# Output stores on GpSimd's software DMA queue, and a first w1 piece of half the size: attention with a soft mixture of experts

## The chip, the cores and the metric

The kernel runs on one core of a Trainium2 chip. The core has a matrix engine (PE, TensorE), three engines for elementwise work (DVE or VectorE, ACT or ScalarE, POOL or GpSimd), and SP (SyncE), which here only issues transfers and waits. Sixteen DMA engines move data between HBM and the on-chip memory SBUF. A transfer can be issued from SP, on a hardware queue, or from POOL, on a software queue, for which POOL itself writes the descriptors. The metric is the device time of one execution in microseconds (us); less is better.

## The reference

The input is `q`, `k`, `v` of shape (8 batches, 8 heads, 576 positions, 64), and weights `moe_phi` (512, 32), `moe_w1` (8, 512, 1024) and `moe_w2` (8, 1024, 512), all float32.

```python
# attention with a mask by head
scores = (q @ k.T) / sqrt(64)
mask_plain = (rel >= 0) & (rel < 32)                       # heads 0..3
mask_dil   = (rel >= 0) & (rel < 128) & (rel % 4 == 0)     # heads 4..7
x = softmax(where(mask, scores, -1e9)) @ v                 # -> (4608, 512)
# soft mixture of experts: 8 experts with 4 slots each
logits = x @ phi
slot_input = softmax(logits, axis=0).T @ x                 # 32 slots
for e in range(8):
    slot_out[e] = relu(slot_input[e] @ w1[e]) @ w2[e]
out = softmax(logits, axis=1) @ slot_out                   # (4608, 512) float32
```

The slots need the logits of all 4608 rows, so no row of the output can be made before the whole attention is done, the experts' weights have been used, and the slot outputs are known.

## The kernel before

The work falls into 16 halves. Half `i` is batch `i // 2` with four of its heads: the plain mask for even `i`, the dilated one for odd `i`. For each half three loads (`load_half`, line 329) bring k, q and v from HBM as float32 and cast them to bf16 on the way. They go into one of four staging sets. DVE turns them (T, line 467 or 473) into one of two working sets, PE computes scores (SC), ACT takes the exponential (EX, line 526), PE and ACT bring v into shape (TB and VE), PE multiplies by v (PV), and DVE normalizes (RC and NM, lines 588 and 592). After that PE and ACT make the transposed x (XT and XE), and once per batch the logits (LG), their exponentials (EXL), their transpose (ET and EE) and the sum for the slots (SI and SA).

The experts' weights are cast to bf16 by the loads too, with one exception. The first 256 rows of `w1[0]`, 1 MB, are read as float32 by SP's hardware queue (line 381) into the space where expert 4's w2 comes later, and ACT casts them in two instructions (line 386). All other weights come through POOL: w1 pieces (line 339), w2 pieces (line 347), and for experts 6 and 7 slabs of 256 columns (line 354), so that the first 256 output columns can be computed before the last slabs are there. `W_AFTER` says how many weight pieces follow the loads of each half on POOL's queue; the rest follow the last half.

The program is not written in the order in which it runs. Each instruction or group is an `op` of a planner (`Sched`) with an engine, a guessed duration, a priority and the buffers it reads and writes. `run` plays them through in modelled time and always takes a ready operation of the least priority value. That gives the order of instructions on each engine; the waits between engines are set by the buffers. A priority in the loop is `PERIOD` times the half's number plus an offset of its stage in `OFFS`. A transfer in the plan has a size and a rate.

Behind the loop come the experts: L1 (line 777) with w1, ReLU on ACT, a transpose, and L2 (line 815) with w2. Their sum goes to `o_so`, first columns 0 to 255, then 256 to 511 (line 837). The output is made in 9 groups of 512 rows: a matmul (`out_tile`, line 856), and an eviction from PSUM to SBUF with the row's scale on ACT (line 865) or DVE (line 868), by turns. `store` (line 876) then sends it to HBM. Groups 0 to 2 are stored in pieces of 256 KB with rows of 1 KB: six pieces of the left columns, then six of the right. Groups 3 to 8 are stored in 1 MB each, 8 KB to a partition. Each store waits for its evictions; SP, which issues them in order, waits for all of them at the end (line 936).

Of the kernel before, what the change touches and what calls it, by code (L numbers as in the profile page):

```python
# [7 lines left out]
ACTF = mybir.ActivationFunctionType  # L8
# [10 lines left out]
NH = 16  # L19


W_AFTER = [0, 1, 1, 1, 1, 1, 1, 1, 1, 1, 1, 1, 1, 1, 1, 99]
PERIOD = 13.0
NSTG = 4
PE_SLOW = 1.1

OFFS = dict(T=12.4, SC=5.3, EX=-0.3, MK=27.3, TB=-8.9, VE=-4.9, PV=-2.7, RC=-36.2, NM=-26.5,
            XT=8.5, XE=14.2, LG=-29.0, EXL=18.1, ET=28.8, EE=6.0, SI=34.4, SA=11.6)


class Buf:
# [22 lines left out]
class Sched:  # L54
# [8 lines left out]
    def op(self, eng, fn, dur, prio, reads=(), writes=(), rmw=(), after=(), banks=(), name="",  # L63
           kind="c", nbytes=0, rate=422e3, lag=0.0, sem=None, tail=False):
        o = Op()
        o.eng, o.fn, o.dur, o.prio, o.name = eng, fn, dur, prio, name
        o.kind, o.bytes, o.rate, o.lag, o.sem, o.tail = kind, nbytes, rate, lag, sem, tail
        o.deps, o.succ = set(), []
        o.banks, o.opens, o.ord = [], [], None
        o.seq = len(self.ops)  # L70
        for a in after:
            if a is not None:
                o.deps.add(a)
        for b in reads:
            o.deps.update(b.w)
            b.r.append(o)
        for b in writes:
            if b.r:
                b.prev = b.w + b.r
                b.w, b.r = [], []  # L80
            o.deps.update(b.prev)
            b.w.append(o)
        for b in rmw:
            o.deps.update(b.prev)
            o.deps.update(b.w)
            o.deps.update(b.r)
            b.w.append(o)
        for b in list(reads) + list(writes) + list(rmw) + list(banks):
            if isinstance(b, Bank) and b not in o.banks:
                o.banks.append(b)  # L90
                if b.left == 0:
                    o.opens.append(b)
                b.left += 1
        o.deps.discard(o)
        self.ops.append(o)
        return o
# [98 lines left out]
def bass_dilated_sliding_attn__then__soft_moe_slots_kernel(  # L195
# [15 lines left out]
    def take(n):  # L211
        o = top[0]
        top[0] = o + (n + 1) // 2 * 2
        return o

    o_w1 = take(8 * 4 * FF)
# [37 lines left out]
    def a(off, dims, p0=0, pn=128):  # L254
        return AP(ar, p0 * NBF + off, [[NBF, pn]] + dims)
# [4 lines left out]
    def af(off, dims, p0=0, pn=128):  # L260
        return AP(ar_f.tensor, (p0 * NBF + off) // 2, [[NBF // 2, pn]] + dims)
# [12 lines left out]
    op = sc.op  # L274
    PE, ACT, DVE, POOL, SP = "PE", "ACT", "DVE", "POOL", "SP"
    pe, act, dve, pool, spq = nc.tensor, nc.scalar, nc.vector, nc.gpsimd, nc.sync

    def pet(n, cols):
        return (40.0 + n * max(cols / 2.4, 27.0)) * PE_SLOW / 1000.0
# [21 lines left out]
    b_w1 = [Buf(f"w1{e}") for e in range(8)]  # L301
    b_w2 = [[Buf(f"w2{e}{s}") for s in range(2)] for e in range(8)]
# [5 lines left out]
    def w2off(e):  # L308
        return o_w2 + e * 8 * DM if e < 5 else o_stg + (e - 5) * 8 * DM


    def sem(n):
        return [nc.alloc_semaphore(n), 0]
# [4 lines left out]
    def dma_in(fn, nbytes, s, prio, name, **kw):  # L318
        o = op(POOL, fn, 0.6, prio, kind="dma", nbytes=nbytes, sem=s,
               name=name, **kw)  # L320
        loads[name] = o
        return o
# [12 lines left out]
    wq = []  # L335

    def w1_piece(e, hf, r0=0, n=2):
        def fn():
            return pool.dma_start(
                a(o_w1 + e * 4096 + hf * 2048 + 1024 * r0, [[1, 1024 * n]]),  # L340
                moe_w1[e, 256 * hf:256 * hf + 256, :].rearrange("(p two) f -> p (two f)", two=2)
                [:, 1024 * r0:1024 * (r0 + n)])
        return (fn, n << 19, f"w1_{e}{hf}", [b_w1[e]])
# [13 lines left out]
        return (fn, n << 17, f"w2s_{e}{s}{c0}", [b_w2[e][s] if n == 8 else b_w2h[c0 // 4][s]])  # L357

    for e in range(8):
        wq += [w1_piece(e, x) for x in range(e == 0, 2)]  # L360
    for e in range(6):
        wq += [w2_piece(e, 0), w2_piece(e, 4)]
    for s in range(2):
# [1 line left out]
    nw = [0]  # L365

    def load_w(n):
        for _ in range(n):
            if nw[0] >= len(wq):
                return  # L370
            fn, nb, name, wr = wq[nw[0]]
            e = int(name.split("_")[1][0])
            rd = []
            if name.startswith("w2") and e >= 5:
                rd = [x for y in b_stg for x in y]
            nw[0] += 1
            dma_in(fn, nb, sem("s_" + name), rate=384e3 if name[2] == "s" else 422e3,
                   lag=2.3 if name[:2] == "w2" else 0.8, prio= -100.0 if nw[0] < 2 else -80.0, name=name, writes=list(wr) + rd)


    op(SP, lambda: spq.dma_start(
        af(w2off(4), [[1, 2048]]),
        moe_w1[0, 0:256, :].rearrange("(p two) f -> p (two f)", two=2)), .1, -200.0,
       kind="dma", nbytes=1 << 20, sem=sem("s_w1f"), writes=b_w2[4], name="w1f")
    for x in range(2):
        op(ACT, lambda x=x: act.activation(
            a(o_w1 + 1024 * x, [[1, 1024]]), af(w2off(4) + 2048 * x, [[1, 1024]]), ACTF.Copy),
            1.1, -200.0, reads=b_w2[4], writes=[b_w1[0]], name=f"w1c{x}")


    def const_ops():
# [50 lines left out]
    for bb in [b_et, b_phis, b_htz, b_sit] + b_p + b_xd + [x for y in b_vb for x in y]:  # L442
# [4 lines left out]
       kind="dma", nbytes=65536, sem=sem("s_phi"), writes=[b_phst], name="phi")  # L447
    for g in range(2):
# [3 lines left out]
           reads=[b_phst], writes=[b_phis])  # L452


    def half(i):
        b, dl = i // 2, i % 2
        T0 = i * PERIOD
        st, kq = i % NSTG, i % 2
        pr = lambda s: T0 + OFFS[s]
        ok, oq, ov = (o_kqv[kq] + 1152 * j for j in range(3))  # L460
# [164 lines left out]
        for x in range(2):  # L625
            bank = Bank(f"xt{i}{x}")

            def xt_fn(x=x, bank=bank):
# [14 lines left out]
            n = 6 if not dl else (2 if x else 8)  # L643
            op(PE, xt_fn, pet(n, 128 if dl else 96), pr("XT") + 0.4 * x, reads=[bx, b_id], writes=[bank],
               name=f"XT{i}{x}")
            c = 2 * dl
# [94 lines left out]
    for i in range(NH):  # L741
        load_half(i)
        half(i)
        if i == 13:
            row_sums(0, 7, 15 * PERIOD)
    names = [w[2] for w in wq]
    load_w(99)
    dma_order, w_at = [], 0
    for i in range(NH):
        dma_order += [f"ld{i}{c}" for c in "kqv"]  # L750
        dma_order += names[w_at:w_at + W_AFTER[i]]
        w_at += W_AFTER[i]
    for x, y in zip(dma_order, dma_order[1:]):
# [7 lines left out]
       writes=[b_rcol], name="cs")  # L761
# [4 lines left out]
       reads=[b_siacc], writes=[b_sit], name="sit")  # L766
    row_sums(7, 9, T1 + 4)
    hs_ops = []
    for g in range(2):
        for x in range(2):  # L770
            bank = Bank(f"l1{g}{x}")

            def l1_fn(g=g, x=x, bank=bank):
# [10 lines left out]
               writes=[bank], name=f"L1{g}{x}")  # L784
# [3 lines left out]
                writes=[b_hsb[g][x], b_p[0], b_p[1]], name=f"RL{g}{x}"))  # L788
    for g in range(2):
        bank = Bank(f"ht{g}")  # L790

        def ht_fn(g=g, bank=bank):
# [10 lines left out]
           reads=[bank], writes=[b_htz], name=f"HE{g}")  # L803
# [5 lines left out]
    def l2(es, x, col, n, cs=range(8), bufs=None):  # L809
# [20 lines left out]
       name="SOx")  # L830
# [14 lines left out]
    store_ops = []  # L845
# [3 lines left out]
    def ostg(G):  # L849
        return o_w1 + 4096 * G if G < 8 else o_w2  # L850
# [21 lines left out]
    def store(G, c0, cw, prio, j0=0, n=4):  # L872
        rd = [b_og[G][j][s] for j in range(j0, j0 + n) for s in range(2)
              if c0 < 256 * (s + 1) and c0 + cw > 256 * s]
        dst = out[512 * G:512 * G + 512, c0:c0 + cw].rearrange("(p j) f -> p j f", j=4)[:, j0:j0 + n, :]
        store_ops.append(op(SP, lambda: spq.dma_start(
            dst, af(ostg(G) + 2 * (512 * j0 + c0), [[512, n], [1, cw]])), .1, prio, kind="dma",
            nbytes=128 * n * cw * 4, rate=347e3 if cw < 512 else 420e3,
            sem=sem(f"s_o{G}{c0}{j0}"), reads=rd, name=f"ST{G}{c0}{j0}"))

    T2 = T1 + 40
    for G in range(NA):
        for x in range(0, 4, 2):
            for j in (x, x + 1):
                out_tile(G, j, 0, 256, T1 + 20 + G + .25 * x)
            store(G, 0, 256, T1 + 20 + G + .25 * x + .2, x, 2)
    for G in range(NA):
        for x in range(0, 4, 2):
            for j in (x, x + 1):
                out_tile(G, j, 256, 256, T2 + 10 + G + .25 * x)  # L890
            store(G, 256, 256, T2 + 10 + G + .25 * x + .2, x, 2)
    for G in range(NA, 9):
        for j in range(4):
            out_tile(G, j, 0, 512, T2 + 10 + G)
        store(G, 0, 512, T2 + 10 + G + .5)
# [74 lines left out]
```

## Time and profile before

| What | Value |
|---|---|
| Time, median of 3 runs | 181.22 us (180.66 to 181.52) |
| The profiled execution's own time | 181.52 us |
| Its span, first to last instruction | 179.7 us |
| Busy: PE, DVE, ACT, POOL | 69%, 64%, 59%, 27% of the span |
| Software queue (loads by POOL) | 30.41 MB written, 14992 packets |
| Hardware queue (SP: w1 piece, phi, stores) | 10.55 MB, 4544 packets |
| HBM read, written | 61.93 MB, 9.44 MB |

The page divides the span into 40 slices of 4.5 us; a digit is the busy share of a slice in tenths. A row of a group or of the timeline names the line of the kernel, the engine, the operation, what it writes and reads, and how many there are. A `q` behind an engine's name means its instruction queue, where transfers are issued. Bytes are counted at the destination, so a load that casts float32 to bf16 counts half of what it reads.

### The profile page before, as it was taken

What the parts mean: (1) busy time and instruction counts of PE and PEld (TensorE: products, weight loads), DVE (VectorE), ACT (ScalarE), POOL (GpSimd) and SP (SyncE); (2) the same over time, 40 slices, a digit from 0 to 9 for tenths busy, and PEclk for the clock granted to TensorE, in tenths of its full rate; (3) what the DMA queues carried; (4) which work ended last, traced back from release to release, by engine and by line L of the source; (5) the groups of instructions that cost most, each with busy time, mean ns of one, the idle gap of its engine ahead of it and who ended that gap; (6) DMA issues with size and microseconds to landing.
All of it is one profiled execution on the core that took longest, in us unless ns stands there. A gap on an engine that the chain in (4) does not pass through costs nothing.

```text
span 179.7 us, 5277 instructions
## 1 busy us (share of the span) xinstructions
PE 123.6 (69%) x2220; PEld 83.7 (47%) x2220; DVE 114.5 (64%) x214; ACT 106.4 (59%) x168; POOL 49.0 (27%) x98
## 2 busy tenths in 40 slices
PE   0018867977889789789689889885696088897000
PEld 0005645755666566566467567673343025531000
DVE  6897779979698698798599599460100013599000
ACT  2406598697799689688678788764141013498000
POOL 7559841432332333232930000930000000000000
PEclk9999999999999999999999999997569969999655
DMA  5999999999999999999999999999999998999994
GB/s 190 233 210 208 216 208 212 212 210 211 215 209 212 214 209 211 214 211 209 214 211 210 214 211 213 215 216 212 215 210 214 196 197 122 330 326 418 410 430 191
DMA packets 19559, 41.30 MB, mean 230 GB/s; under 512 B 1872, under 2 KB 9040, under 8 KB 18640
## 3 DMA queue, kind: packets, MB, share of 16 engines
q0 software_dynamic: 14992, 30.41, 89.7%
q1 hardware_dynamic: 4544, 10.55, 15.5%
q8 instruction: 18, 0.29, 0.6%
q14 instruction: 5, 0.04, 0.1%
HBM read 61.93 MB, written 9.44 MB: 397 GB/s over the span
## 4 chain that ended last, share of the span: by engine, by line
DMA 58%; DVE 19%; PE 10%; issue 3%; ACT 1%; DVEq 0%; POOL 0%; POOLq 0%
DMA ar<-in_k_dram 41%; DMA ar<-in_moe_w_dram 17%; DVE ar L868 5%; DVE ar L467 5%; PE ps L815 5%; DVE ar L592 2%; PE ps L487 2%; DVE ar L427 2%; PE ps L856 1%; DVE ar L432 1%; PE ps L494 1%; PE ps L548 1%; ACT ar L648 1%; ACT ar L526 1%; DVE ar L473 1%
## 5 line engine op out<-in xcount | busy, mean ns | idle before, releaser
L467 DVE STREAM_TRANSPOSE ar<-ar 128x576 uint32<-128x576 uint32 x40 | 48.9, 1244 | 10.1 <-DMA ar<-in_k_dram 10.0
L526 ACT ACTIVATE ar<-ps 128x1152 bf16<-128x1152 f32 (+1 forms) x32 | 38.1, 1190 | 19.8 <-PE ps L511 10.6
L487 PE MATMUL ps<-ar 128*128 128x320 bf16 (+1 forms) x128 | 22.8, 302 | 15.8 <-DVE ar L467 12.7
L554 ACT ACTIVATE ar<-ps 128x768 bf16<-128x768 bf16 x32 | 25.0, 812 | 4.3 <-PE ps L548 3.8
L592 DVE TENSOR_TENSOR ar<-ps,fs 96x768 bf16<-96x768 f32 (+1 forms) x32 | 26.2, 821 | 1.2
L548 PE MATMUL ps<-ar 128*128 128x128 bf16 x192 | 15.8, 228 | 6.4 <-DVE ar L592 4.3
L487 PEld LDWEIGHTS ps<-ar 128*128 128x128 bf16 x128 | 10.6, 99 | 20.1 <-POOL ar L400 12.6
L581 PE MATMUL ps<-ar 128*128 128x65 bf16 x320 | 14.9, 193 | 2.3 <-ACT ar L526 1.8
L548 PEld LDWEIGHTS ps<-ar 128*128 128x128 bf16 x192 | 12.1, 118 | 8.8 <-issue 4.0
L329 POOL DMA_DIRECT2D ar<-in_k_dram x16 | 8.9, 556 | 23.5 <-DVE ar L467 13.1
L865 ACT ACTIVATE ar<-ps,fs 128x256 f32<-128x256 f32 (+1 forms) x24 | 11.5, 619 | 6.1 <-PE ps L856 6.1
L581 PEld LDWEIGHTS ps<-ar 128*128 128x128 bf16 x320 | 12.2, 97 | 4.7 <-ACT ar L526 2.2
L815 PE MATMUL ps<-ar 128*32 128x512 bf16 (+1 forms) x80 | 10.0, 386 | 6.1 <-DMA ar<-in_moe_w_dram 4.4
L868 DVE TENSOR_SCALAR ar<-ps,fs 128x256 f32<-128x256 f32 (+1 forms) x24 | 12.8, 607 | 1.1 <-PE ps L856 1.1
L347 POOL DMA_DIRECT2D ar<-in_moe_w_dram x12 | 6.4, 580 | 21.0 <-DVE ar L467 21.0
L856 PE MATMUL ps<-ar 128*128 128x256 bf16 (+1 forms) x48 | 10.5, 334 | 1.8 <-DVE ar L837 1.1
L329 POOL DMA_DIRECT2D ar<-in_v_dram x16 | 8.8, 549 | 10.6 <-DVE ar L467 5.9
L329 POOL DMA_DIRECT2D ar<-in_q_dram x16 | 8.8, 548 | 10.0 <-DVE fs L588 5.7
L588 DVE RECIPROCAL fs<-ps 96x12 f32<-96x12 f32 (+1 forms) x32 | 6.3, 197 | 7.9 <-PE ps L581 7.2
L671 PE MATMUL ps<-ar 128*128 128x288 bf16 x64 | 9.9, 301 | 1.9 <-ACT ar L655 1.8
L648 ACT ACTIVATE ar<-ps 128x576 bf16<-128x576 bf16 x16 | 9.7, 656 | 2.3 <-PE ps L632 2.2
L815 PEld LDWEIGHTS ps<-ar 128*32 128x32 bf16 x80 | 4.8, 104 | 11.1 <-issue 9.1
(68 smaller groups left out, 180.3 us busy)
## 6 DMA issues: line engine op xcount, KB each, us to landing
ar<-in_moe_w_dram POOLq DMA_DIRECT2D x29, 512.0 KB, 27.2
out_dram<-ar SPq DMA_DIRECT2D x6, 1024.0 KB, 9.8
ar<-in_k_dram POOLq DMA_DIRECT2D x16, 288.0 KB, 23.5
ar<-in_q_dram POOLq DMA_DIRECT2D x16, 288.0 KB, 23.8
ar<-in_v_dram POOLq DMA_DIRECT2D x16, 288.0 KB, 23.8
out_dram<-ar SPq DMA_DIRECT2D x12, 256.0 KB, 3.1
ar<-in_moe_w_dram SPq DMA_DIRECT2D x1, 1024.0 KB, 5.1
ar<-in_moe_w_dram POOLq DMA_DIRECT2D x4, 256.0 KB, 34.7
```

Of the source, the lines that this page charges most:

```text
L329: return pool.dma_start(a(o_stg + (s * 3 + j) * 1152, [[1, 1152]]), src[b, 4 * dl:4 * dl + 4].rearrange("h (p t) d -> (h p) (t d)", p=32))
L467: return dve.transpose(au(o_dst, [[1, 18], [18, 32]]), au(src, [[32, 18], [1, 32]]))
L487: pe.matmul(pf(h, 0, [[1, W]]), a(o_id, [[1, 128]]), a(msk, [[1, W]]), start=True, stop=False)
L526: eo = op(ACT, lambda P=P, W=W: act.activation(a(P, [[W, 4], [1, W]]), AP(ps, 0, [[4096, 128], [512, 4], [1, W]]), ACTF.Exp, scale=SCALE), ...
L548: last = pe.transpose(pb(bank.idx, bb * 256 + par * 32, [[64, 4], [1, 32]]), src, a(o_id, [[1, 128]]))
L554: op(ACT, lambda t=t, bank=bank: act.activation(a(o_vb[vs] + 3 * t * VBK, [[66, 12], [2, 32], [1, 2]]), pb(bank.idx, 0, [[64, 12], [1, 32] ...
L581: last = pe.matmul(pf(bank.idx + x, 65 * t, [[1, 65]]), w, a(VB + t * VBK + 66 * h, [[1, 65]]), start=True, stop=True)
L592: op(DVE, lambda hp=hp, bank=bank: dve.tensor_tensor(a(ox + 128 * hp, [[64, 2], [256, NT], [1, 64]], 0, rows), pf(bank.idx, 0, [[512, 2], ...
L815: last = pe.matmul(pf(sobank[x].idx, 0, [[1, n]], 32 * j, 32), a(o_htz + 1024 * g + 128 * c + 32 * j, [[1, 32]]), a(w2off(e) + DM * c + co ...
L856: op(PE, lambda: pe.matmul(pf(bank.idx, 0, [[1, cw]]), a(o_et + 512 * G + j, [[4, 128]]), a(o_so + c0, [[1, cw]]), start=True, stop=True), ...
L865: op(ACT, lambda: act.activation(dst, src(), ACTF.Copy, scale=sca), actt(cw, .1), prio + .1, reads=[bank, b_rinv], writes=wr, name=f"OE{G} ...
L868: op(DVE, lambda: dve.tensor_scalar(dst, src(), sca, None, op0=AluOp.mult), dvet(cw, True), prio + .1, reads=[bank, b_rinv], writes=wr, na ...
```

## The change

The output stores are issued by POOL instead of SP, with other durations and rates for the planner. SP's first load fetches only the first of the two 4 KB rows that each partition needs, 0.5 MB, and ACT casts it in one instruction; the other rows come as a piece of their own on POOL's queue. Two weight pieces instead of one follow half 1's loads, and both may be issued among the first. The offsets of the stages in the plan have other values.

```diff
-W_AFTER = [0, 1, 1, 1, 1, 1, 1, 1, 1, 1, 1, 1, 1, 1, 1, 99]
+W_AFTER = [0, 2, 1, 1, 1, 1, 1, 1, 1, 1, 1, 1, 1, 1, 1, 99]
...
-OFFS = dict(T=12.4, SC=5.3, EX=-0.3, MK=27.3, TB=-8.9, VE=-4.9, PV=-2.7, RC=-36.2, NM=-26.5,
-            XT=8.5, XE=14.2, LG=-29.0, EXL=18.1, ET=28.8, EE=6.0, SI=34.4, SA=11.6)
+OFFS = dict(T=11.1, SC=0.6, EX=1.0, MK=13.2, TB=-8.2, VE=-1.3, PV=-27.6, RC=-28.0, NM=-27.1,
+            XT=-13.0, XE=1.8, LG=-37.3, EXL=16.9, ET=26.7, EE=14.5, SI=23.9, SA=8.8)
...
     for e in range(8):
-        wq += [w1_piece(e, x) for x in range(e == 0, 2)]
+        wq += [w1_piece(e, 0, 1, 1) if e == 0 else w1_piece(e, 0), w1_piece(e, 1)]
...
-                   lag=2.3 if name[:2] == "w2" else 0.8, prio= -100.0 if nw[0] < 2 else -80.0, name=name, writes=list(wr) + rd)
+                   lag=2.3 if name[:2] == "w2" else 0.8, prio= -100.0 if nw[0] < 3 else -80.0, name=name, writes=list(wr) + rd)
...
     op(SP, lambda: spq.dma_start(
-        af(w2off(4), [[1, 2048]]),
-        moe_w1[0, 0:256, :].rearrange("(p two) f -> p (two f)", two=2)), .1, -200.0,
-       kind="dma", nbytes=1 << 20, sem=sem("s_w1f"), writes=b_w2[4], name="w1f")
-    for x in range(2):
-        op(ACT, lambda x=x: act.activation(
-            a(o_w1 + 1024 * x, [[1, 1024]]), af(w2off(4) + 2048 * x, [[1, 1024]]), ACTF.Copy),
-            1.1, -200.0, reads=b_w2[4], writes=[b_w1[0]], name=f"w1c{x}")
+        af(w2off(4), [[1, 1024]]),
+        moe_w1[0, 0:256, :].rearrange("(p two) f -> p two f", two=2)[:, 0, :]), .1, -200.0,
+       kind="dma", nbytes=1 << 19, sem=sem("s_w1f"), writes=b_w2[4], name="w1f")
+    op(ACT, lambda: act.activation(a(o_w1, [[1, 1024]]), af(w2off(4), [[1, 1024]]), ACTF.Copy),
+       1.1, -200.0, reads=b_w2[4], writes=[b_w1[0]], name="w1c")
...
-        store_ops.append(op(SP, lambda: spq.dma_start(
-            dst, af(ostg(G) + 2 * (512 * j0 + c0), [[512, n], [1, cw]])), .1, prio, kind="dma",
-            nbytes=128 * n * cw * 4, rate=347e3 if cw < 512 else 420e3,
+        store_ops.append(op(POOL, lambda: pool.dma_start(
+            dst, af(ostg(G) + 2 * (512 * j0 + c0), [[512, n], [1, cw]])), .6, prio, kind="dma",
+            nbytes=128 * n * cw * 4, rate=400e3 if cw < 512 else 427e3,
             sem=sem(f"s_o{G}{c0}{j0}"), reads=rd, name=f"ST{G}{c0}{j0}"))
```

## The prediction

> **What bounds the kernel now.** I read the page's slices first, then the DMA queues and issues, then the chain of waits, and last the two ends of the run in short windows. The page:
>
> ```profile
> DMA  5999999999999999999999999999999998999994
> GB/s 190 233 210 208 216 208 212 212 210 211 215 209 212 214 209 211 214 211 209 214 211 210 214 211 213 215 216 212 215 210 214 196 197 122 330 326 418 410 430 191
> ...
> q0 software_dynamic: 14992, 30.41, 89.7%
> q1 hardware_dynamic: 4544, 10.55, 15.5%
> ...
> DMA 58%; DVE 19%; PE 10%; issue 3%; ACT 1%; DVEq 0%; POOL 0%; POOLq 0%
> ...
> out_dram<-ar SPq DMA_DIRECT2D x6, 1024.0 KB, 9.8
> ar<-in_k_dram POOLq DMA_DIRECT2D x16, 288.0 KB, 23.5
> ```
>
> The DMA engines are 90% busy in every slice but the first, one near 150 us, and the last. Loads write bf16 and read f32, so 212 GB/s written is 424 GB/s read. The k loads land 23.5 us after their issue: the software queue is that far ahead of the compute, and no other engine sets the pace. The chain of waits says the same: 58% of it is transfers. So time can change in three ways: DMA work, a hole in it, or a shift of its ends. Now the start (columns of a window: length, busy time of PE, PEld, DVE, ACT, POOL, granted clock, DMA share, GB/s):
>
> ```profile
> 3.00:3.50 0.50, 0.00 (x0) 0.00 (x0) 0.36 (x1) 0.00 (x0) 0.50 (x3) 1.00 0.97 410
> ...
> 4.50:5.00 0.50, 0.00 (x0) 0.00 (x0) 0.50 (x6) 0.00 (x0) 0.50 (x2) 1.00 0.93 371
> 5.00:5.50 0.50, 0.00 (x0) 0.00 (x0) 0.23 (x2) 0.00 (x0) 0.50 (x3) 1.00 1.14 238
> ```
>
> By the queues of each window, until 5.0 us only the hardware queue moves (w1f), and the first six packets of the software queue come in 5.00 to 5.25. Their load was issued at 1.24. And the end:
>
> ```profile
> 143.62 3.59 PE L815 MATMUL ps<-ar 128*32 128x512 bf16 x16 [4.44 <-DMA ar<-in_moe_w_dram]
> ...
> 152.00 15.12 SPq L876 DMA_DIRECT2D out_dram<-ar  x18
> ```
>
> ```profile
> 152.00:153.00 1.00, 0.91 (x7) 0.50 (x8) 1.00 (x3) 1.00 (x4) 0.00 (x0) 1.00 0.22 42
> 153.00:154.00 1.00, 0.92 (x8) 0.58 (x6) 0.93 (x3) 0.67 (x2) 0.00 (x0) 1.00 1.06 332
> ...
> 157.00:158.00 1.00, 0.97 (x6) 0.39 (x5) 1.00 (x4) 1.00 (x5) 0.00 (x0) 1.00 0.81 278
> ...
> 178.00:179.00 1.00, 0.00 (x0) 0.00 (x0) 0.00 (x0) 0.00 (x0) 0.00 (x0) 0.50 0.06 25
> ```
>
> Queues of 153 to 154:
>
> ```profile
> q1 hardware_dynamic: 330, 0.32, 98.7%
> q0 software_dynamic: 19, 0.01, 6.9%
> ```
>
> The slice near 150 us lies between loads and stores. The last big w2 piece lands at 143.4; L2, the sum and the first output tiles follow in a chain without a further DMA wait; the first store is issued at 152.00. Loads thin out from 150; the last 19 packets after 153 are one engine's share (6.9% of sixteen), so one DMA engine ends its loads at about 153.7, and again one engine's share, 0.06, is all that still moves in 178 to 179; I take it for the same engine. All later work of this engine lies in a row. So the end is: 153.7, plus stores of 256 columns (3.15 MB at the 347 GB/s of 154 to 157, 9.1 us), plus 1 MB stores (6.29 MB at the 418 of 163 to 177, 15.0 us) = 177.8; seen 178.9, the last 1.1 being instruction fetches and what I cannot place; the span ends 0.8 later. This execution took 181.52, with 1.8 outside its span, and is 0.30 over the median of 181.22.
>
> **The change part by part.**
>
> *Half of w1f moves to the software queue.* HBM reads are the same 61.9 MB. SP's first DMA falls from 1 MB to 0.5 MB; POOL issues one DMA more (the group's mean, 0.54 us) before its constants, where it idles 3.96 us on DVE's L437 later: nothing. ACT loses one of two casts (2.00 us for both, at 5.87, with ACT then idle until 14.42): nothing. On the DMA engines the hardware work ends 0.524 MB / 410 GB/s = 1.3 us sooner, near 3.7, and phi's 64 KB after it near 4.2. If the software queue can start by then, the total is unchanged: 0. If its 5.0 start was its own delay, there is a hole of 0.9. For readiness speaks that at 153 to 154 one engine ran 19 software packets at 41 ns each while hardware stores were already moving on the others: an engine drains one queue before the other. Bound of a warm start: the load issued at 12.78 came behind 6 x 288 KB + 512 KB = 2.29 MB, which from 5.1 at 211 GB/s lasts to 16.0, and shares in 15 to 18 are 1.09, 1.02, 1.11, with no hole: issue to data is at most 3.2 us, so ready by 4.4. I take +0.1, ends 0 and +0.9.
>
> *Orders by the new offsets.* The order of instructions on PE and DVE differs in halves 1 to 5; from there on only the second TB of each even half stands later, behind XT and SI. The last 60 rows of PE agree, those of DVE but for one swap. The loads' 23.5 us of lead hides it: 0. If that lead were used up, each us of stall would show whole.
>
> *Second w1 piece in W_AFTER.* Puts 1.5 MB instead of 1 MB ahead of half 2's loads, as 0.5 MB less is on the other queue: 0, hidden by the same lead.
>
> *Stores move from SP to POOL.* All 18 issues and their DMAs go to the software queue, behind all loads; POOL's last load is issued by 118.4, so nothing is queued behind a waiting store but other stores; SP keeps the final wait. An issue costs SP 0.45, POOL 0.55 to 0.9 by its load groups; six of 0.6 take 3.6 us, against 4.0 for their data: hidden. Three terms remain.
>
> (a) Issue to first data, L. SP: issued at 152.00, 20 packets before 153.0, hence about 0.9 us. POOL: between that and 3.2. I take 1.5, nearer the hardware row, since the longer one only says where a full queue did not run dry. The first six stores do not feel it: the late engine is at its loads until 153.7. The next six do: SP issues the first at 156.82, so data can come at 156.82 + L = 158.3; before, the late engine came to them at 153.7 + 1.573 MB / 347 = 158.2. So +0.1; L = 0.9 makes it 157.7 (then the engine's own end of the first six decides), -0.5; L = 3.2 makes 160.0, +1.8.
>
> (b) Rows of 1 KB. Hardware stores run at 347 GB/s. The software queue's nearest row is the w2 slabs, 1 KB read to 512 B written, 197 GB/s from 144 to 149, 394 of reads. At 394 the first six end sooner, 153.7 + 4.0 = 157.7, which (a) has used; the second six save 1.573/0.347 - 1.573/0.394 = 0.54. Ends: 0 (a store of 1 KB is 1 KB whoever issues it) and -0.54. I take -0.54, as the queue differs in these rows where 8 KB rows do not.
>
> (c) Rows of 8 KB: 418 stored against 414 to 428 read by the software queue (207 to 214 written): 0, ends +0.15 and -0.3.
>
> Sum: 0.1 + 0.1 - 0.54 + 0 = -0.34; 181.52 - 0.34 = 181.18 for this execution, **180.9** for the median.
>
> Two rules weigh on (a). The row: POOL's first seven loads took 0.54 to 0.68 us each while DVE wrote memsets throughout, no longer than later ones. The Trainium skill, "SBUF — State Buffer", "SBUF: two separate sides", says that GpSimd cannot write descriptors while VectorE runs an operation that takes the shared port, and gives 620 ns alone against 3100 under one; by it, as an estimate, the second six would start 2.5 us later and the sum be +2.2. No run here shows it, and the output evictions read PSUM. The skill's "DMA: Bandwidth & Descriptors", "Latency and other measured facts", gives about 1 us to the first byte for the software path and 0.6 for the hardware one; with that 0.4 on top of the 0.9 seen, the second six would start at 158.1 and the sum be -0.5.
>
> **Rivals**, priced against the median. *Slower: a slow start of the software queue.* L of 2.9 or more (start hole 1.24 + L - 4.2, second stores 156.82 + L - 158.2, less 0.54) makes over +0.9. For it: 3.9 us between the first issue and the first data. Against: the hardware queue filled that time to the end. Price at L = 3.2 and with the start hole of 0.9: 0.9 + 1.8 - 0.54 = +2.2, 183.4.
>
> *Faster: the software queue starts like the hardware queue.* L = 0.9, no hole, slab rate, 8 KB rows at 428: -0.5 - 0.54 - 0.3 = -1.3, 179.9.
>
> *The rate does not change.* 1 KB stores cost 46 ns an engine on either queue: with L = 1.5 then 0.1 + 0.1, +0.2, 181.4.
>
> *The loop starves or descriptors are blocked.* Price 2 or more; against it the lead and the issue times above.
>
> **How the numbers follow.** Forecast with the unchanged rate: 0.46, own range 180.4 to 181.9. Faster rival 0.27. Slow start 0.20, starving or blocking 0.07. About 0.5% (0.9 us) is what a measurement can tell from no change; the forecast lies inside it. Faster 0.27, same 0.46, slower 0.27. The range, 179.8 to 182.9, takes in the faster case whole and the slow ones up to L near 3.
>
> **What would show it.** Software packets by 4.3 with no window under 0.9 in 3.5 to 5.5 (start); share at the 1 KB stores with 390 or more GB/s (b); issue to first store data and a dip near 157 to 158 of about 0.5 us (a); 8 KB at 410 to 428 (c); first store issue at 152.0. Wrong would make it: that issue elsewhere, as when the half clock at 143 to 147, in which L815's 16 matmuls took 3.59 us, falls otherwise; stores of the software queue cut into other pieces; a late completion of its last store.

## The result, and the profile after

The changed kernel takes 185.85 us (median, 185.45 to 186.29) against 181.37 us for the kernel before, measured beside it (180.66 to 181.87). The ratio is 1.0251 with an interval of 1.0208 to 1.0293: slower, by 4.5 us. It lies above the whole predicted range. Below, a time is the median of all executions of a kernel, and its ratio is to the kernel before, run beside it (medians of 181.6 to 182.3 there), without the executions on either side that fell in a second, slower state.

The profiled execution of the changed kernel took 186.29 us with a span of 184.0; the one before took 181.52 with 179.7. The difference of 4.77 us divides as follows. A landing is the last of the sixteen completion signals of a transfer in the trace; for these two stores it comes 0.35 us after the last packet has ended (178.93 before, 180.24 after).

| Step, us from the start of the span | Before | After | Difference |
|---|---|---|---|
| Last store has landed | 179.28 | 180.59 | +1.31 |
| SP has seen it and begins its DRAIN at the end of the program | 179.51 | 180.82 | (+1.31) |
| POOL's DRAIN ends | 157.39 | 183.74 | |
| From SP's DRAIN to the end of the span | 0.22 | 3.15 | +2.93 |
| Time outside the span | 1.79 | 2.32 | +0.53 |

First, the page's slices and DMA queues after (each digit or figure is a slice of 4.6 us):

```profile
DMA  5999999999999999999999999999999997999990
GB/s 130 203 209 211 219 206 211 214 209 214 212 212 210 215 209 211 214 212 209 213 211 212 211 215 214 216 209 213 214 214 202 197 173 200 309 355 406 417 388 5
...
q0 software_dynamic: 16960, 40.11, 102.1%
q1 hardware_dynamic: 416, 0.59, 1.3%
...
out_dram<-ar POOLq DMA_DIRECT2D x6, 1024.0 KB, 10.6
ar<-in_k_dram POOLq DMA_DIRECT2D x16, 288.0 KB, 24.1
```

Everything but phi and the half w1 piece is now on the software queue. The loop is as full as before, and the k loads still land some 24 us after their issue. What is new stands at the right edge: the last slice is empty. The 12 stores of 1 KB rows make far fewer packets than before (16960 and 416 on the two queues, against 14992 and 4544). The end of the run shows what the empty slice is. These are the windows after (length, busy time of PE, PEld, DVE, ACT, POOL, granted clock, DMA share, GB/s):

```profile
178.00:179.00 1.00, 0.00 (x0) 0.00 (x0) 0.00 (x0) 0.00 (x0) 0.00 (x0) 0.50 0.85 352
179.00:180.00 1.00, 0.00 (x0) 0.00 (x0) 0.00 (x0) 0.00 (x0) 0.00 (x0) 0.50 0.24 98
180.00:181.00 1.00, 0.00 (x0) 0.00 (x0) 0.00 (x0) 0.00 (x0) 0.00 (x0) 0.50 0.00 0
...
183.00:184.00 1.00, 0.00 (x0) 0.00 (x0) 0.00 (x0) 0.00 (x0) 0.00 (x0) 0.50 0.00 0
```

From 180.6 on nothing moves and no engine computes, and yet the span lasts to 184.0. SP's waits after (waiter, releaser: us in total, times, longest) give that stretch a name, although a misleading one:

```profile
SPq L934 <- DMA out_dram<-ar: 178.7, 9, 161.4
SPq L938 <- PEq L938: 3.1, 1, 3.1
```

Line 938 is the end of the program's block, where all engines meet. Before, the same wait (line 940) was:

```profile
SPq L940 <- PEq L940: 0.2, 1, 0.2
```

PE is only the last link of the meeting. Which engine came late is told by the DRAIN that each engine's queue runs before it. This is the group of instructions of that line after (line, engine, operation, count: minimum/median/maximum in ns, first and last start in us):

```profile
L938 POOLq EVENT_SEMAPHORE  x2: 17/17/17, 183.8 to 183.9; - x2
L938 PEldq DRAIN  x1: 460/460/460, 164.7 to 164.7; - x1
L938 ACTq DRAIN  x1: 737/737/737, 164.7 to 164.7; - x1
L938 DVEq DRAIN  x1: 1514/1514/1514, 165.1 to 165.1; - x1
L938 POOLq DRAIN  x1: 16663/16663/16663, 167.1 to 167.1; - x1
L938 SPq DRAIN  x1: 7/7/7, 180.8 to 180.8; - x1
```

and before:

```profile
L940 POOLq DRAIN  x1: 41819/41819/41819, 115.6 to 115.6; - x1
...
L940 SPq DRAIN  x1: 7/7/7, 179.5 to 179.5; - x1
```

POOL's DRAIN runs from its last instructions until some time after its last transfer. Before, its record started at 115.57, beside the last three issues, and ended at 157.39, 3.35 us after the last load had landed (154.03), and 22 us before SP was done: it cost nothing. After, the last software transfer is the last store. The DRAIN ends at 183.74, 3.15 us after that store's landing, and the program waits for it.

The other part, the landing that is 1.31 us later, can be read from the bytes that were still to be stored at 163. The DMA queues in the window 163 to 182, before and then after (packets, MB, share of the sixteen engines in the window):

```profile
q1 hardware_dynamic: 836, 5.99, 76.2%
```

```profile
q0 software_dynamic: 959, 6.57, 85.4%
```

The change leaves 0.58 MB more for the last stretch; at the 415 GB/s of 166 to 178 that is 1.4 us, about the lateness of the landing. So this part is lost while the small stores run, and none that can be seen with the 1 MB stores.

### The profile page after: what moved, and what is told of

Read it like the earlier page. It is cut to its first block, busy times and chain, and to the rows that moved or that the text cites. A ratio compares the mean times of both kernels' runs of the same rounds, so it can differ in the third digit from the quotient of the medians.

```text
span 184.0 us, 5283 instructions
## 1 busy us (share of the span) xinstructions
PE 125.2 (68%) x2220; PEld 85.6 (47%) x2220; DVE 113.7 (62%) x214; ACT 105.8 (57%) x167; POOL 61.3 (33%) x117
## 3 DMA queue, kind: packets, MB, share of 16 engines
q0 software_dynamic: 16960, 40.11, 102.1%
## 4 chain that ended last, share of the span: by engine, by line
DMA 44%; DVE 22%; PE 15%; issue 4%; ACT 3%; POOL 1%; POOLq 0%; DVEq 0%
DMA ar<-in_k_dram 28%; DMA ar<-in_moe_w_dram 16%; DVE ar L465 7%; PE ps L813 4%; DVE ar L866 4%; DVE ar L590 3%; PE ps L485 3%; PE ps L546 2%; DVE ar L425 1%; ACT ar L646 1%; ACT ar L524 1%; PE ps L492 1%; PE ps L854 1%; DVE ar L471 1%; DVE ar L430 1%
## 5 line engine op out<-in xcount | busy, mean ns | idle before, releaser
L874 POOL DMA_DIRECT2D out_dram<-ar x18 | 11.8, 658 | 37.0 <-DVE ar L866 35.1
L485 PEld LDWEIGHTS ps<-ar 128*128 128x128 bf16 x128 | 10.6, 100 | 20.9 <-POOL ar L398 12.6
L546 PE MATMUL ps<-ar 128*128 128x128 bf16 x192 | 16.3, 234 | 4.3 <-DVE ar L590 4.0
L546 PEld LDWEIGHTS ps<-ar 128*128 128x128 bf16 x192 | 12.8, 121 | 5.8 <-DVE ar L590 2.2
L579 PEld LDWEIGHTS ps<-ar 128*128 128x128 bf16 x320 | 12.3, 99 | 6.3 <-issue 4.2
```

The source lines that it names most:

```text
L485: pe.matmul(pf(h, 0, [[1, W]]), a(o_id, [[1, 128]]), a(msk, [[1, W]]), start=True, stop=False)
L546: last = pe.transpose(pb(bank.idx, bb * 256 + par * 32, [[64, 4], [1, 32]]), src, a(o_id, [[1, 128]]))
L579: last = pe.matmul(pf(bank.idx + x, 65 * t, [[1, 65]]), w, a(VB + t * VBK + 66 * h, [[1, 65]]), start=True, stop=True)
L874: store_ops.append(op(POOL, lambda: pool.dma_start(dst, af(ostg(G) + 2 * (512 * j0 + c0), [[512, n], [1, cw]])), .6, prio, kind="dma", nby ...
```

## The experiments

The theory after the comparison: POOL's DRAIN cannot end before about 3.2 us after the last software transfer, and this end, not the speed of the stores, is the larger part of the loss. The rivals: the software queue simply stores more slowly, or starts late, and the end of the program only follows; the half w1 piece and the offsets cost something in the loop; the wait at the end belongs to late transfers of any queue; or POOL's DRAIN has a length of its own, whether transfers are on the way or not.

**The parts of the change apart.** First all stores on POOL, and nothing else of the change (the kernel before with this edit; here and below, the planner's duration and rate of a store go with its issuer):

```diff
-        store_ops.append(op(SP, lambda: spq.dma_start(
+        store_ops.append(op(POOL, lambda: pool.dma_start(
...
```

> The kernel before with only the stores moved to POOL; first w1 piece and offsets as before. Drain theory: 2.9 us of drain, 0.4 outside the span and about 1.1 of slower small stores come with the stores alone: about 185.5. Rival, that the start (4 KB rows on the hardware queue, and the offsets) costs the most: about 182.

It took 185.62 us, a ratio of 1.0233 (1.0169 to 1.0297). The last store landed at 180.01, and the DRAIN ended at 183.16, again 3.15 us later:

```profile
L940 POOLq DRAIN  x1: 16283/16283/16283, 166.9 to 166.9; - x1
...
L940 SPq DRAIN  x1: 7/7/7, 180.3 to 180.3; - x1
```

Then the rest of the change without the stores (the changed kernel with its stores back on SP):

```diff
-        store_ops.append(op(POOL, lambda: pool.dma_start(
+        store_ops.append(op(SP, lambda: spq.dma_start(
...
```

> The changed kernel with all stores back on SP: the half w1 piece, W_AFTER and the new offsets are left. The run with small stores on POOL and large ones on SP was 0.7% over the kernel before. If that rest is the start (4 KB rows on the hardware queue moved 0.5 MB in the time of most of 1 MB): about 182.2. If it is the small stores' slower way through POOL: about 181.5.

181.84 us, 1.0008 (0.9961 to 1.0054). The half w1 piece, the second piece in `W_AFTER` and the offsets of the stages cost nothing that can be measured, though the interval reaches up to 1.0 us. As far as the times tell, the loss belongs to the stores.

**Only the small stores on POOL.** In the changed kernel the six stores of 1 MB go back to SP:

```diff
+        onp = cw < 512
-        store_ops.append(op(POOL, lambda: pool.dma_start(
+        store_ops.append(op(POOL if onp else SP, lambda: (pool if onp else spq).dma_start(
...
```

> The changed kernel, with its six 1 MB stores issued by SP again and the twelve 256 KB stores still on POOL. Drain theory: POOL's last software transfer lands near 166, its drain at the end of the block is over near 169, long before the last store lands, so the 2.9 us between SP's last wait and the end go away, and with them the extra 0.4 outside the span: about 182.5. Rival, that stores on the software queue are slow to start and to run: nearly all of that is in the small stores, which stay, so about 185.5.

182.54 us, 1.007 (1.0026 to 1.0114). The DRAIN's end moved back under cover: POOL's last store landed at 169.28, its DRAIN ended at 172.51 (3.23 later), and SP's last landing at 180.19 sets the end again:

```profile
L939 POOLq DRAIN  x1: 12591/12591/12591, 159.9 to 159.9; - x1
...
L939 SPq DRAIN  x1: 7/7/7, 180.4 to 180.4; - x1
```

```profile
SPq L939 <- PEq L939: 0.2, 1, 0.2
```

Of the 2.5% of the whole change, 0.7% are left. The rest goes away with the last six stores, though their own speed was not the trouble. The same with nothing else of the change (the kernel before, with `onp = cw < 512` in its store):

> The kernel before with only the twelve 256 KB stores on POOL. If the rest of the loss is in the small stores: about 182.4, with the first store data near 153.7 instead of 152.9 and about 300 GB/s behind it. If it is the start: about 181.6.

183.15 us, 1.0063 (1.0004 to 1.0123), with the DRAIN ending at 170.63, again 3.23 us after the small stores had landed. Both point to some 0.6 to 0.7%, 1.1 to 1.3 us, that small stores through POOL cost of themselves, though the second interval nearly reaches 1.

**Only the last store on POOL.** The kernel before, with one store of 18 moved:

```diff
+        onp = G == 8
-        store_ops.append(op(SP, lambda: spq.dma_start(
+        store_ops.append(op(POOL if onp else SP, lambda: (pool if onp else spq).dma_start(
...
```

> The kernel before with one store of eighteen, the last 1 MB, issued by POOL. Drain theory: one software transfer that lands last is enough for the whole drain, 2.9 us and 0.4 outside the span: about 184.6, with a POOL drain that ends about 3.2 us after that store landed. Rival, slow software stores: one store issued 10 us ahead of its data costs nothing, 181.4.

Four executions gave 181.36, 185.11, 184.48 and 185.34. The profiled one was the 181.36, which looked like a miss; of the other three there is no trace. In this trace the DRAIN comes last all the same. The software store was issued after all of SP's (165.52, SP's last at 164.00), but landed at 175.95, before SP's last (177.65). The DRAIN ended at 179.35 (3.40 later), and SP waited for it 1.6 us. The time is as short as before only because all the stores of this execution were early: the first was issued at 150.13, against 152.00 before. I ran the same kernel again:

> The kernel with the last 1 MB store on POOL once more, for its profile. Its runs spread from 181.4 to 185.3, and the profiled one was the shortest: there the software store landed at 175.95, before two hardware stores issued ahead of it, and the drain was over at 179.35. If the software store lands last this time, near 179.5, the drain should end near 182.8 and the time be about 184.7; if it lands early again, 181.4.

184.24 us in one execution. Here the first store was issued at 153.28. The software store landed at 178.74, again before SP's last (180.54), and the DRAIN ended at 182.13, again 3.40 later, while SP was done at 180.84:

```profile
L941 POOLq DRAIN  x1: 13937/13937/13937, 168.2 to 168.2; - x1
...
L941 SPq DRAIN  x1: 7/7/7, 180.8 to 180.8; - x1
```

The software store landed 2.8 us later than in the execution before it, as all the stores did; the distance from its landing to the DRAIN's end was the same. In both traces this one store cost 1.3 to 1.4 us beyond the moment when SP was done, and not the whole 2.9, because it landed 1.7 to 1.8 us before SP's last. The 2.9 us between the two times go with stores that began 3.1 us apart, long before the one on POOL was issued. The control is the same edit with the first of the 1 MB stores, `onp = G == 3`:

> The kernel before with the first 1 MB store on POOL instead of the last. Drain theory: it lands near 166, the drain is over by 170, nothing shows: 181.6. Rival, that a 1 MB store on the software queue is itself slow or disturbs the others: as much as the last one cost, 184.5.

181.30 us, 0.9977 (0.9931 to 1.0023). That store landed at 169.25 and the DRAIN ended at 172.65: hidden, and the kernel is as fast as before. This 1 MB store by POOL, which lands 9.7 us before SP's last, costs nothing that can be measured.

**A repair that failed.** The changed kernel with its last two 1 MB stores on SP (`onp = G < 7`) was meant to hide the DRAIN and keep the rest:

> The changed kernel with the last two 1 MB stores on SP, sixteen on POOL. Drain theory: the last software transfer should land about 5 us ahead of the end if the two queues were served one after the other, so its drain would be hidden, about 182.7; if they are served together the software stores land near the end too, and part of the drain shows, up to 185.5. Rival, slow software stores: 185.5 in any case.

186.61 us, 1.0264 (1.0191 to 1.0338): no gain. In the profiled execution (188.2 us) POOL's last store landed at 182.94, later than SP's at 182.61, and the DRAIN ended at 186.17. The DMA engines served the two queues side by side, so that POOL's last store was not early although it was issued first (167.61, against 168.46 and 169.71 for SP's two). The hope rested on an order between queues that this trace does not show; the theory of the DRAIN holds (3.23 us after the landing, and 2.9 after SP was done at 183.29). The execution is long for another reason too: its first store was issued at 154.40, against 152.40 in the trace of the changed kernel.

**A late transfer that nobody needs.** The kernel before keeps all its stores on SP, and gets a load of 64 KB, read by nobody, on POOL, issued once the store of group 7 has landed:

```diff
+    store_ops.append(op(POOL, lambda: pool.dma_start(
+        f(o_phst, [[64, 2], [1, 64]]),
+        moe_phi.rearrange("(hf p two) s -> p hf (two s)", hf=2, two=2)), .6, 1e6, kind="dma",
+        nbytes=65536, sem=sem("s_late"), after=[x for x in store_ops if x.name == "ST700"],
+        writes=[b_phst], name="late"))
```

> The kernel before, all stores on SP, with one useless software load added: POOL reads the 64 KB of phi again into the space that held it, once the last store but one has landed (near 177). It should land near 179.5, with or just after the last store. Drain theory: the POOL drain ends about 3.2 us after that load has landed, near 182.7, and the time is about 184.6 though no store uses the software queue. Rival, slow software stores: no store is slow here, so at most 0.3 for the load itself, 181.9.

186.61 us, 1.0262 (1.017 to 1.0354): a useless load of 64 KB costs as much as the whole change. But the distance did not fit. The load landed at 178.13, and the DRAIN ended at 183.27, 5.14 us later instead of 3.2 to 3.4:

```profile
175.79 0.71 POOL L897 DMA_DIRECT2D fs<-in_moe_phi_dram  x1 [56.81 <-DMA out_dram<-ar]
```

```profile
L945 POOLq DRAIN  x1: 7500/7500/7500, 175.8 to 175.8; - x1
...
L945 SPq DRAIN  x1: 7/7/7, 178.4 to 178.4; - x1
```

The same load on SP, as control:

> The same useless load at the same place, issued by SP on the hardware queue: the control of the run with the software load. Both theories expect at most 0.3 over the kernel before, about 181.9, with the POOL drain over near 157.

182.01 us, 1.002 (0.9965 to 1.0074). So it is not a late load as such; it has to be POOL's.

The odd 5.14 us needed another reading. Perhaps POOL's DRAIN has a length of its own. To see it without any transfer, the kernel before got a memset of one column on POOL at the same place, when the software queue had been empty for more than 20 us:

```diff
+    op(POOL, lambda: pool.memset(f(o_phst, [[1, 1]]), 0.0), .2, 1e6,
+       after=[x for x in store_ops if x.name == "ST700"], writes=[b_phst], name="late")
```

> The kernel before with one useless memset of a single column on POOL, placed as late as the useless load was (after the last store but one has landed, near 177). The software queue has been empty since 154. If the drain waits for outstanding software transfers and their clean-up alone: the drain starts near 177 and ends at once, time as before. If every drain of POOL takes some us from its own start, whatever the queue holds: it ends 3 to 7 us after 177, and the time is 183 to 186.

186.06 us, 1.0232 (1.0111 to 1.0353). The theory in its strict form, in which the DRAIN waits for transfers alone, fell. The memset took 0.10 us, and SP was done at 178.90, but POOL's DRAIN lasted until 183.10. The timeline of POOL, then the group of instructions at the block's end, of this kernel:

```profile
176.30 0.10 POOL L897 MEMSET fs<- 128x1 f32 x1 [58.25 <-DMA out_dram<-ar]
```

```profile
L942 POOLq DRAIN  x1: 6822/6822/6822, 176.3 to 176.3; - x1
...
L942 SPq DRAIN  x1: 7/7/7, 178.9 to 178.9; - x1
```

```profile
SPq L942 <- PEq L942: 4.4, 1, 4.4
```

A DRAIN of POOL takes 6.8 us even with nothing on its way on the software queue. Its record overlaps POOL's last instruction, here the memset, so that it ends 6.7 us after that instruction has ended. In the kernel with the useless load it lasts 7.50 us and overlaps an issue of 0.71, and so it ends 6.8 us after that issue. So the useless load paid for being POOL's last instruction, and not for its landing. If that is right, the same memset costs nothing when it comes two stores earlier (`"ST500"`):

> The useless memset of one column on POOL two stores earlier, after the store of group 5 has landed (near 170.5 to 172). The late memset's drain ended 6.7 us after the memset, with the software queue empty since 154. If a drain takes 6.7 us from POOL's last instruction: it is over near 178, SP's last wait near 179.5 decides, time as before. If the late memset cost what it did because the drain also waits for the last hardware store: it ends some 4.4 us after that store landed, near 183.5, and the time is 185.5 again.

180.91 us, 0.9944 (0.989 to 0.9999). The DRAIN is as long, and ends at 178.95, before SP is done. It does not wait for SP's stores either, which would have been another reading of the late memset: the last of them landed at 179.32, after the DRAIN's end:

```profile
L942 POOLq DRAIN  x1: 6815/6815/6815, 172.1 to 172.1; - x1
...
L942 SPq DRAIN  x1: 7/7/7, 179.6 to 179.6; - x1
```

The interval ends at 0.9999; with a program that only adds a memset I don't take this for a gain. The useless load one store earlier (`"ST600"`) was meant to move between the two:

> The useless software load one store earlier (after the store of group 6 has landed, near 174.5 at the latest), landing near 176. In the run with the load one store later the drain ended 5.1 us after the landing, 7.5 after its start, against 3.2 to 3.4 after the landing elsewhere. If the end follows the landing by 5.1 for this load: drain over near 181, about 1.3 later than before, 182.9. If by 3.3: over near 179.3, 181.6.

185.92 us, 1.0225 (1.0119 to 1.033): it hid less than hoped. The load shared the DMA engines with the stores and landed only at 179.06; the DRAIN ended at 182.45, 3.40 after that landing, while SP was done at 179.29. Here the landing decides, and not POOL's own 6.7 us.

The kernels together, with the later of the two bounds in bold (us; "own end" is the end of POOL's last instruction plus 6.7):

| Kernel | Last software landing | Landing to DRAIN's end | POOL's own end | DRAIN's end | SP done |
|---|---|---|---|---|---|
| Before | **154.03** | 3.35 | 125.1 | 157.39 | 179.51 |
| Changed | **180.59** | 3.15 | 174.3 | 183.74 | 180.82 |
| All stores on POOL, nothing else | **180.01** | 3.15 | 174.1 | 183.16 | 180.25 |
| Small stores on POOL, the rest of the change | **169.28** | 3.23 | 167.9 | 172.51 | 180.43 |
| Last store on POOL, second execution | **178.74** | 3.40 | 175.5 | 182.13 | 180.84 |
| Useless load after group 7 | 178.13 | 5.14 | **183.2** | 183.27 | 178.37 |
| Useless load after group 6 | **179.06** | 3.40 | 181.7 | 182.45 | 179.29 |
| Memset after group 7 | empty since 153.5 | – | **183.1** | 183.10 | 178.90 |
| Memset after group 5 | no late transfer | – | **178.9** | 178.95 | 179.56 |

No kernel in this study beats the one before.

## Why the prediction was wrong

**The step that failed: the end of the program.** The prediction wrote that "SP keeps the final wait" and closed its account with the landing of the last store ("the span ends 0.8 later"). It asked what stands behind each store on POOL's queue and found only other stores. It did not ask what POOL itself does after them. In the trace of before there was a row of 41.8 us for it, POOL's DRAIN, whose end lay 3.35 us behind the last software landing. It was off the path, and I had not read the rows at the block's end at all. This is worth +2.9 of the 4.8 us. None of the rivals had it; "a late completion of its last store" came nearest among the things that would make the forecast wrong, though the store's completion was seen by SP 0.23 us after the landing, as before.

**The start (+0.1; ends 0 and +0.9): no hole, but perhaps too small.** The software queue moved its first packets at 3.75 us, where 4.4 had been the bound. Windows after, with the columns as above:

```profile
3.00:3.50 0.50, 0.00 (x0) 0.00 (x0) 0.36 (x1) 0.00 (x0) 0.50 (x2) 1.00 0.92 205
3.50:4.00 0.50, 0.00 (x0) 0.00 (x0) 0.50 (x1) 0.00 (x0) 0.50 (x2) 1.00 1.37 276
4.00:4.50 0.50, 0.00 (x0) 0.00 (x0) 0.50 (x2) 0.00 (x0) 0.50 (x2) 1.00 0.69 148
4.50:5.00 0.50, 0.00 (x0) 0.00 (x0) 0.50 (x6) 0.00 (x0) 0.50 (x2) 1.00 0.94 176
5.00:5.50 0.50, 0.00 (x0) 0.00 (x0) 0.23 (x2) 0.33 (x1) 0.50 (x2) 1.00 1.11 199
```

The 0.69 lies under the 0.9 that the prediction named as a sign, but it follows 1.37, and the mean of the two is 1.03: there is no hole. The estimate that the hardware queue would be done 1.3 us sooner was too kind, as its piece in 4 KB rows moved at 205 GB/s where the one in 8 KB rows had 410. And the loads came later: the w1 piece with which the same bytes have been read in both kernels landed at 17.72, against 17.20 before. At the other end, the last load landed at 154.03 to 154.46 in the four traces with the new start, and at 153.18 to 153.62 in the ten experiments with the old one (154.03 in the trace of before itself). So the term may be nearer its upper end, +0.9. The run with only this part, 1.0008 with an interval of −0.7 to +1.0 us, cannot tell +0.1 from that.

**Orders, offsets, `W_AFTER` (0): nothing seen against it**, by the same run and with the same interval. The last big w2 piece, read from the start of L2's matmuls, came within 0.25 us of before:

```profile
143.85 3.31 PE L813 MATMUL ps<-ar 128*32 128x512 bf16 x16 [4.73 <-DMA ar<-in_moe_w_dram]
```

**(a) Issue to first data (+0.1; ends −0.5 and +1.8): the size of L nearly right, its effect too small.** The timeline of POOL after:

```profile
152.40 4.28 POOL L874 DMA_DIRECT2D out_dram<-ar  x6 [33.57 <-DVE ar L866]
157.19 5.34 POOL L874 DMA_DIRECT2D out_dram<-ar  x8 [0.50 <-DVE ar L866]
```

POOL issues its first store 0.4 us after SP would have (152.00), its first data moves at 153.71, 1.3 us after the issue, and L had been put at 1.5. The 0.4 us belong to the change too: counted from the end of the DVE eviction before the first store (151.97 before, 151.92 after), SP issues 0.03 us later and POOL 0.48, and the first data moves 0.94 us later by SP and 1.79 by POOL. The prediction then said that the first six stores "do not feel it", since one DMA engine was at its loads until 153.7, and that an issue of 0.6 us was hidden. One engine of sixteen was; the other fifteen had been storing since 153 under SP. And an issue took 0.71 us, so six 256 KB stores come at 367 GB/s at best (4.28 us for 1.57 MB), while the windows show that the engines were short of work:

```profile
153.00:154.00 1.00, 0.87 (x8) 0.54 (x7) 0.88 (x3) 0.63 (x2) 1.00 (x3) 1.00 0.43 129
154.00:155.00 1.00, 0.92 (x7) 0.61 (x8) 0.00 (x0) 0.00 (x0) 1.00 (x2) 1.00 0.82 283
155.00:156.00 1.00, 0.48 (x5) 0.20 (x4) 0.43 (x1) 0.00 (x0) 1.00 (x3) 1.00 0.89 283
```

Before, 153 to 154 had a share of 1.06 and 332 GB/s. By 158 SP's queue had stored 1.66 MB, POOL's about 1.32: 0.34 MB, or 0.8 us at 415 GB/s, against the +0.1 of the sum.

**(b) Rows of 1 KB (−0.54; ends 0 and −0.54): the gain did not come.** The prediction took the rate of loads with 1 KB rows for the rate of stores with 1 KB rows. Queues in 154 to 157, before and then after:

```profile
q1 hardware_dynamic: 1079, 1.04, 103.9%
```

```profile
q0 software_dynamic: 265, 0.89, 90.1%
```

The software queue packs four rows of 1 KB into one packet of 4096 bytes, but that packet takes 191 ns where four of 1 KB took 46 ns each, 184. By these lines a full share would carry 0.33 MB per us on either queue (0.89/3/0.901 and 1.04/3/1.039). The stores were cut into other pieces than before, which the prediction had named as a danger, but the rate did not move by it. The rival "the rate does not change" had this term right. On top of it the share stayed lower in the second six too (158 to 163: 1.55 MB at a share of 0.94, against 1.79 at 1.04), which makes another 0.24 MB, 0.6 us. So (a) and (b) together gave +1.4 where the sum had −0.44; the run with the small stores alone, +0.6% or 1.1 us (0.1 to 2.2), agrees.

**(c) Rows of 8 KB (0): right**, 415 GB/s from 166 to 178 against 418 from 163 to 177 before.

**The two rules.** Descriptor writing was not blocked: POOL's stores took 0.53 to 0.73 us each while DVE evicted output tiles. So the long price in the Trainium skill, "SBUF — State Buffer", "SBUF: two separate sides", did not come into play; the evictions read PSUM, and no run here puts a DVE operation of the kind that the page names beside the issues of stores. The skill's "DMA: Bandwidth & Descriptors", "Latency and other measured facts", gives about 1 us to the first byte by the software path and 0.6 by the hardware one. The difference of 0.4 is borne out, counted from the issue: 1.3 us here against 0.9 by SP.

**What stays open.** No run shows whether the later loads of the new start reach the end of the program. The time outside the span grew by 0.53 us in the profiled execution of the changed kernel and by 0.28 with all stores on POOL alone, but stayed at 1.8 to 1.9 in other kernels whose DRAIN came last; no run here settles it. That POOL's DRAIN consists of a fixed part, a wait for its transfers and another fixed part is inferred from the two bounds; the trace has only the one row.

## What to carry to other kernels

Before moving transfers to another engine's queue, read what each engine does between its last instruction and the end of the program: an engine that finishes early hides a long DRAIN, and giving it the last piece of work brings that DRAIN onto the path. In this kernel POOL's last software transfer has to land 3.4 us, and its last instruction to end some 7 us, before the last store of another queue; even a memset of 0.10 us cost 2.3% (1.1 to 3.5) when it was POOL's and last. And a wait that the profile lays to one engine at a barrier may only name the last link: the DRAIN rows of the barrier's line show who came late.

## What the runs showed of the hardware

- POOL's DRAIN at the end of the program lasts 6.82 us when nothing is on its way on the software queue (0.10 of it beside the memset before it); those of PE, ACT, DVE and SP at the same place last 0.46, 0.74, 1.51 and 0.007 us. With software transfers outstanding it ends 3.15 to 3.40 us after the last one has landed, in eleven kernels. In a twelfth, whose last load landed 1.6 us after its issue was over, it ends 5.14 us after the landing, because the 6.8 us from POOL's last instruction last longer.
- The software queue stores four rows of 1 KB as one packet of 4096 bytes, in 191 ns, and gains no time by it.
- Stores on the two queues do not land in the order of their issue. A store that POOL issued after all of SP's landed before SP's last (175.95 against 177.65 in one execution, 178.74 against 180.54 in another), and one that POOL issued before SP's last two landed after both (182.94 against 178.07 and 182.61).
- The hardware queue read w1 rows of 4 KB at 205 GB/s in 3.0 to 3.5 us, and rows of 8 KB at 410 in the same window of the kernel before, each with a share of over 0.9.
